# One load of 32 KB rows for the keys of unit 1 in the first and the last pair, instead of two of 16 KB rows

## The chip, the cores and the metric

The kernel runs on one core of a Trainium2 chip. A core has five engines with a queue of instructions each: TensorE (PE in the profile, its weight loads PEld), VectorE (DVE), ScalarE (ACT), GpSimd (POOL) and SyncE (SP). They work side by side and wait for each other by semaphores. Data comes from the chip's memory by DMA: an engine, here nearly always SP, issues a load, 16 DMA engines carry it out, and its semaphore reaches 16 when the last of them is done. The metric is the time of one execution on the device in microseconds (us), as the median of several.

## The reference

One step of attention decoding: 32 query heads share 8 key and value heads (4 queries each), over 65,536 positions with 128 elements each, in bfloat16.

```python
B, Hq, Hkv, Sq, Sk, D = 1, 32, 8, 1, 65536, 128
k = jnp.repeat(k, rep, axis=1)          # rep = 4
v = jnp.repeat(v, rep, axis=1)
scores = jnp.einsum("bhqd,bhkd->bhqk", q, k) * scale
p = _softmax(scores, axis=-1)
return jnp.einsum("bhqk,bhkd->bhqd", p, v)
```

Keys and values are 134 MB each, and each byte is used once for the four queries of its head.

## The kernel before

**Units and pairs.** The positions of a head are cut into 4 units of 16,384, so that there are 32 units. A unit lies in SBUF as 128 partitions by 128 tiles of 128 elements: each partition holds 128 consecutive positions, 32 KB per partition and 4 MB in all. Two units make a pair, p = 0 to 15. In a pair, unit n = 0 of the keys lies in the first half of `kbuf`, and unit 1 in `bbuf`, from which PE reads it; `vbuf` has room for both units of the values.

**Loads** (`sync_engine`, L393 to L447). SP issues all loads of keys and values, in order of pairs, keys before values. For pairs 1 to 13 (`WHOLE`) one load of 64 KB rows brings both units of keys into `kbuf` (L413), and POOL and ACT copy unit 1 from there to `bbuf` in pieces of 16 tiles (`copy_unit`, L204). For pairs 0, 14 and 15 the two units are loaded apart, and unit 1 goes straight to `bbuf`. In pairs 0 and 15 each of these loads is cut into pieces of `K_PIECES` tiles (`pieces`, L400; a tile is 256 bytes of a partition's row, so 64 tiles make rows of 16 KB). Each piece has its own semaphore, `kp[n][i]`; where there are no pieces, one load serves piece 0 and SP raises the other semaphores itself (`tokens`, L404). The values come in one load per pair of 64 KB rows, except in pair 0 (two of 32 KB rows) and in pair 15, where unit 1 comes in pieces of 73, 38, 13 and 4 tiles (`V_PIECES`).

Before a load SP waits until its place is free: `kfree` (L411), `bfree` (L418, for pairs 14 and 15), and `vfree` (L428), which DVE raises when PE has done the values of the pair before (L291, L303).

**PE** (`pe_pair`, L165). For each unit PE works in 16 groups of 8 tiles: it transposes a group of keys through the identity into PSUM (`pe_transposes`, L124; L132), and three groups later (`LAG`) multiplies the transposed keys by the four queries (`pe_scores`, L135; L141). DVE evicts three of four transposed groups from PSUM to `ktb` (L202), ACT the fourth (L200). The stream runs on from unit 0 into unit 1 without a break: the last scores of unit 0 stand behind the first transposes of unit 1. At the first group of a piece PE takes that piece's semaphore (L126, L127). After both units follow the values, 128 matmuls each (`pe_values`, L146; L159), unit 0 and then unit 1. In the last pair a correction matmul adds the accumulated sum ahead of tile 73 of unit 1 (L152).

**Between scores and values** DVE takes a maximum per partition and POOL one over the partitions, ACT computes the exponentials (L342), and DVE rescales the running sum and adds the values of a unit when PE has done them (L254).

The lines that the change bears on, of the kernel before:

```python
K_PIECES = ((64, 64), (64, 64))                                             # L23
        if j * TB in starts(K_PIECES[n]):                                   # L126, on PE
            take(pe, kp[n][starts(K_PIECES[n]).index(j * TB)], 16)
            for a, w, sm in zip(starts(sizes), sizes, sems):                # L401, on SP
                e.dma_start(to[:, a * D:(a + w) * D], s[:, a * D:(a + w) * D]).then_inc(sm, 16)
                    if p in (0, NP - 1):                                    # L420, on SP
                        pieces(to, s, K_PIECES[n], kp[n])
```

Of the kernel before, what the change touches and what calls it, by code (L numbers as in the profile page):

```python
# [19 lines left out]
Q = 32  # L20


K_PIECES = ((64, 64), (64, 64))  # L23
V_PIECES = ((128,), (73, 38, 13, 4))


# [12 lines left out]
def starts(sizes):  # L39
    return [sum(sizes[:i]) for i in range(len(sizes))]  # L40


def take(e, sem, n=1):

    e.wait_ge(sem, n)
    e.sem_inc(sem, -n)  # L46


def bass_standalone__gqa_softmax__decode_kernel(nc, q, k, v, out):
# [16 lines left out]
    def sem(name):  # L66
        return S(nc.semaphore(name))
# [36 lines left out]

    kp = [[sem(f"kp{i}_{p}") for p in range(len(K_PIECES[i]))] for i in range(2)]
    vp = [[sem(f"vp{i}_{p}") for p in range(len(V_PIECES[i]))] for i in range(2)]
# [17 lines left out]
    def pe_transposes(pe, n, j):  # L124
        kv = (bbuf if n else kbuf)[:, 0:T * D].rearrange("p (t d) -> p t d", d=D)
        if j * TB in starts(K_PIECES[n]):  # L126
            take(pe, kp[n][starts(K_PIECES[n]).index(j * TB)], 16)  # L127
        if n and j * TB % CB == 0:
# [264 lines left out]
    def sync_engine(e):  # L393
# [6 lines left out]
        def pieces(to, s, sizes, sems):  # L400
            for a, w, sm in zip(starts(sizes), sizes, sems):  # L401
                e.dma_start(to[:, a * D:(a + w) * D], s[:, a * D:(a + w) * D]).then_inc(sm, 16)  # L402
# [5 lines left out]
        for p in range(NP):  # L408
# [6 lines left out]
            else:  # L415
                for n in range(2):
# [3 lines left out]
                    if p in (0, NP - 1):  # L420
                        pieces(to, s, K_PIECES[n], kp[n])
                    else:
# [62 lines left out]
```

## Time and profile before

| what | value |
|---|---|
| median of 3 runs | 628.26 us (628.15 to 628.27) |
| the profiled execution, its own time | 628.49 us |
| its span, first to last instruction | 627.1 us |
| read from memory | 268.44 MB |
| busy share of the span: PE, DVE, ACT, POOL | 77%, 50%, 36%, 25% |
| mean granted clock of PE | 0.77 |

The profile is of one execution. Its page has the busy share of each engine in 40 equal slices of the span (a digit is tenths, 9 is 90% or more), the granted clock of PE in the same slices, a chain of waits followed back from the end, groups of instructions by line, and the DMA issues with the median time from issue to landing. The trace behind it can be asked for a timeline of one engine (start, duration, engine, line, operation, output<-inputs, count; in brackets the idle time before it and what ended it), for the DMA issues of a short stretch alone, and for stretches of time (for each engine busy time and count of instructions, then the granted clock, the DMA share and GB/s). Times of the trace count from the span's start.

### The profile page before, as it was taken

The page shows a single profiled execution, that of the slowest core. Times are in us where ns is not written, and L with a number is a line of the kernel's source. Part 1 is how long each engine was busy: PE and PEld are TensorE (multiplying, and loading weights), DVE is VectorE, ACT ScalarE, POOL GpSimd, SP SyncE. Part 2 cuts the span into 40 slices and gives each one's busy share as a digit, 9 for nine tenths or more (in the row PEclk, how much of TensorE's full clock was granted, in tenths as well). Part 3 has the DMA queues.
Part 4 walks back from the last instruction along what each step waited for, and adds up shares of the span by engine and source line. Part 5 has one row for each costly group of instructions (what it writes and reads, how often), then busy time and mean ns, then how long its engine had stood idle before and what let it go on. Part 6 is the DMA issues. An engine that isn't in the chain of part 4 may idle for free. (4 is left out here: it accounts for less than half of the span.)

```text
span 627.1 us, 27836 instructions
## 1 busy us (share of the span) xinstructions
PE 485.4 (77%) x12292; PEld 479.7 (76%) x12292; DVE 315.0 (50%) x699; ACT 228.9 (36%) x445; POOL 159.9 (25%) x124
## 2 busy tenths in 40 slices
PE   4851995949959498695976949779496895999797
PEld 4851995949859498695976949779496895999697
DVE  4620653717537174371744617356182562848283
ACT  2320542515335153341634406245071441624142
POOL 0000704307042070520605115060250702400000
PEclk9865886958869597695977959779596795969596
DMA  8999999999999999999999999999999999999997
GB/s 368 433 454 424 439 431 439 426 443 426 443 418 451 414 447 418 443 422 439 431 431 439 426 439 431 439 431 435 435 435 435 435 435 435 416 451 428 402 436 308
DMA packets 6568, 268.57 MB, mean 428 GB/s; under 512 B 928, under 2 KB 1056, under 8 KB 1184
## 3 DMA queue, kind: packets, MB, share of 16 engines
q1 hardware_dynamic: 6512, 268.45, 99.2%
q8 instruction: 6, 0.10, 0.1%
q10 hardware_dynamic: 48, 0.01, 0.0%
q14 instruction: 2, 0.02, 0.0%
HBM read 268.44 MB, written 0.01 MB: 428 GB/s over the span
## 5 line engine op out<-in xcount | busy, mean ns | idle before, releaser
L202 DVE COPY ktb<-trb 128x1024 bf16<-128x1024 bf16 x384 | 254.6, 689 | 177.3 <-PE trb L132 173.4
L132 PE MATMUL trb<-ident,kbuf 128*128 128x128 bf16 x2048 | 179.0, 246 | 105.4 <-PEq L46 105.3
L200 ACT ACTIVATE ktb<-trb 128x1024 bf16<-128x1024 bf16 x128 | 131.0, 1023 | 351.7 <-PE trb L132 297.5
L132 PEld LDWEIGHTS trb<-ident,kbuf 128*128 128x128 bf16 x2048 | 145.4, 112 | 106.4 <-issue 106.1
L208 POOL COPY bbuf<-kbuf 128x2048 bf16<-128x2048 bf16 x78 | 143.9, 1892 | 178.2 <-POOLq L46 178.2
L141 PE MATMUL qkb<-qcur,ktb 128*128 128x4 bf16 x4096 | 174.4, 165 | 11.0 <-PEq L46 10.0
L141 PEld LDWEIGHTS qkb<-qcur,ktb 128*128 128x128 bf16 x4096 | 155.8, 97 | 16.0 <-issue 16.0
L132 PE MATMUL trb<-ident,bbuf 128*128 128x128 bf16 x2048 | 157.0, 220 | 3.2 <-issue 3.2
L159 PE MATMUL pvb<-pts,vbuf 128*128 128x4 bf16 x4096 | 113.3, 166 | 15.2 <-issue 8.8
L159 PEld LDWEIGHTS pvb<-pts,vbuf 128*128 128x128 bf16 x4096 | 111.4, 103 | 16.9 <-issue 15.5
L132 PEld LDWEIGHTS trb<-ident,bbuf 128*128 128x128 bf16 x2048 | 117.3, 97 | 1.1 <-issue 1.1
L388 POOL PARTITION_ALL_REDUCE cmaxa<-cmax x32 | 11.9, 370 | 252.6 <-POOLq L46 252.6
L342 ACT ACTIVATE pts<-qkb,negm 128x128 bf16<-128x128 f32 x128 | 51.0, 549 | 37.2 <-ACTq L46 37.2
L351 ACT ACTIVATE bbuf<-kbuf 128x2048 bf16<-128x2048 bf16 x26 | 49.5, 1902 | 0.0
L342 ACT ACTIVATION_READ_ACCUMULATOR pts<-qkb,negm 128x1 f32 x128 | 35.6, 278 | 0.0
L220 DVE TENSOR_REDUCE cmax<-qkb 128x4 f32<-128x512 f32 x32 | 22.0, 686 | 23.2 <-DVEq L46 23.2
L254 DVE TENSOR_TENSOR acc<-acc,pvb 128x4 f32<-128x4 f32 x16 | 2.5, 159 | 31.2 <-PE pvb L159 31.2
L252 DVE COPY acc<-pvb 128x4 f32<-128x4 f32 x8 | 1.3, 163 | 20.1 <-PE pvb L159 20.1
L390 POOL PARTITION_ALL_REDUCE la<-lp x8 | 3.4, 430 | 30.8 <-POOLq L46 30.8
L231 DVE SCALAR_TENSOR_TENSOR negm<-cmaxa,m 128x4 f32<-128x4 f32 x24 | 3.9, 164 | 11.7 <-DVEq L46 11.5
L346 ACT ACTIVATE alpha<-dm 128x4 f32<-128x4 f32 x32 | 7.1, 221 | 0.0
L245 DVE TENSOR_TENSOR acc<-acc,alpha 128x4 f32<-128x4 f32 x24 | 3.9, 164 | 6.1 <-DVEq L46 5.7
(42 smaller groups left out, 39.0 us busy)
## 6 DMA issues: line engine op xcount, KB each, us to landing
vbuf<-in_v_dram SPq DMA_DIRECT2D x3, 4096.0 KB, 31.0
kbuf<-in_k_dram SPq DMA_DIRECT2D x4, 2048.0 KB, 16.1
bbuf<-in_k_dram SPq DMA_DIRECT2D x4, 2048.0 KB, 21.0
kbuf<-in_k_dram SPq DMA_DIRECT2D x1, 4096.0 KB, 16.3
bbuf<-in_k_dram SPq DMA_DIRECT2D x1, 4096.0 KB, 16.5
vbuf<-in_v_dram SPq DMA_DIRECT2D x1, 2336.0 KB, 27.1
vbuf<-in_v_dram SPq DMA_DIRECT2D x1, 1216.0 KB, 29.6
vbuf<-in_v_dram SPq DMA_DIRECT2D x1, 416.0 KB, 30.2
```

The costliest lines, as they stand in the source:

```text
L132: ins = pe.transpose(trb[j % NTB][:, i * P:(i + 1) * P], kv[:, t, :], ident[:, :])
L141: ins = pe.matmul(qkb[n][:, t * R:(t + 1) * R], lhsT=ktb[:, off:off + P], rhs=qcur[:, :], start=True, stop=True)
L159: ins = pe.matmul(pvb[n][:, 0:R], lhsT=vv[:, t, :], rhs=pts[n][:, t * R:(t + 1) * R], start=t == 0, stop=t == T - 1)
L200: e.activation(dst, trb[j % NTB][:, :], AF.Copy).then_inc(eva, 1)
L202: e.tensor_copy(dst, trb[j % NTB][:, :]).then_inc(evd, 1)
L208: ins = op(bbuf[:, c * CB * D:(c + 1) * CB * D], kbuf[:, off:off + CB * D])
L220: e.tensor_reduce(cmax[:, :], qkb[n][:, :].rearrange("p (t g) -> p g t", g=R), AX.X, ALU.max).then_inc(cm, 1)
L231: return e.scalar_tensor_tensor(to[:, :], cmaxa[:, :], -scale, mo[:, :], ALU.mult, ALU.min)
L342: ins = e.activation(pv[:, g, :], sv[:, g, :], AF.Exp, bias=negm[:, g:g + 1], scale=scale, accum_out=rsum[:, g:g + 1])
L346: e.activation(alpha[:, :], dm[:, :], AF.Exp, scale=1.0).then_inc(sx, 1)
L351: return e.activation(o, i, AF.Copy)
L388: e.partition_all_reduce(cmaxa[:, :], cmax[:, :], P, bass.bass_isa.ReduceOp.max).then_inc(cma, 1)
```

## The change

`K_PIECES` has one piece of 128 tiles for unit 1 instead of two of 64:

```diff
-K_PIECES = ((64, 64), (64, 64))
+K_PIECES = ((64, 64), (128,))
 V_PIECES = ((128,), (73, 38, 13, 4))
```

In pairs 0 and 15 SP issues one load of 4 MB with rows of 32 KB into `bbuf` where it issued two of 2 MB with rows of 16 KB. There is one semaphore for it, `kp[1][0]`, which PE takes ahead of the first transposes of unit 1, in every pair; the second one, which PE took ahead of group 8 of unit 1, is gone, and with it SP's increments of it in the other pairs. On SP the list of loads differs at these two places alone; the instructions of PE, DVE, ACT and POOL are in the same order.

## The prediction

> **What bounds the kernel now.** I read the page's summary first, for what is busy all the time:
>
> ```profile
> span 627.1 us, 27836 instructions
> PE   4851995949959498695976949779496895999797
> DMA  8999999999999999999999999999999999999997
> HBM read 268.44 MB, written 0.01 MB: 428 GB/s over the span
> ```
>
> The DMA row is 9 in all slices but the first and the last. PE has slices of 4 and 5 in every pair, until the last eight slices. So the load queue sets the pace, and PE can catch up with it in every pair but the last, after which no load follows that could cover it. Next I read the chain of waits, for the end:
>
> ```profile
> 585.89 6.98 PE pvb L159 x256
> ...
> 593.79 29.62 DMA vbuf<-in_v_dram
> ...
> 623.46 1.69 PE pvb L159 x55
> ```
>
> The chain says that the end waits for a V load. How near PE is to being the one that is late shows only in PE's own timeline of the last 23 us:
>
> ```profile
> 592.92 3.57 PE L132 MATMUL trb<-ident,kbuf 128*128 128x128 bf16 x32
> ...
> 604.39 0.61 PE L132 MATMUL trb<-ident,bbuf 128*128 128x128 bf16 x8
> ...
> 616.05 0.34 PE L141 MATMUL qkb<-qcur,ktb 128*128 128x4 bf16 x8 [0.52 <-PEq L46]
> 616.36 3.50 PE L159 MATMUL pvb<-pts,vbuf 128*128 128x4 bf16 x128
> 620.75 2.09 PE L159 MATMUL pvb<-pts,vbuf 128*128 128x4 bf16 x73 [0.89 <-PEq L46]
> 622.70 0.57 PE L152 MATMUL pvb<-acc,identf 128*128 128x4 f32 x2
> 623.46 1.68 PE L159 MATMUL pvb<-pts,vbuf 128*128 128x4 bf16 x55 [0.19 <-DMA vbuf<-in_v_dram]
> ```
>
> The reader is to see the 0.19 in the last row. From 592.92 on PE works without a gap that a DMA causes: both transposed units, their scores, the values of unit 0, the first 73 tiles of unit 1. It is done with them at 622.70 + 0.57 = 623.27, and waits 0.19 us for the second V piece. The kernel is bound by loads for 623 us, yet whatever delays PE in the last pair by more than 0.19 us moves the end. The two short gaps (0.52 and 0.89) end with PE's own chain (scores, maximum, exponentials, values), so they move along with a delay and don't absorb it.
>
> **The change, part by part.** Two things change: how fast the loads go, and when unit 1's keys may be read.
>
> *Loads.* Four 2 MB loads (the two halves of unit 1's keys, in pairs 0 and 15) become two of 4 MB. What one costs in the full queue is the distance of landings; landing is issue plus time to landing:
>
> ```profile
> 580.56 0.80 SPq L402 DMA_DIRECT2D bbuf<-in_k_dram  x2
> bbuf<-in_k_dram SPq DMA_DIRECT2D x1, 2048.0 KB, 19.7
> L402 SPq DMA_DIRECT2D bbuf<-in_k_dram x1: 433/433/433, 580.9 to 580.9; - x1
> bbuf<-in_k_dram SPq DMA_DIRECT2D x1, 2048.0 KB, 24.3
> 592.94 2.23 SPq L402 DMA_DIRECT2D vbuf<-in_v_dram x5
> vbuf<-in_v_dram SPq DMA_DIRECT2D x1, 4096.0 KB, 21.9
> ```
>
> The first half lands at 580.56 + 19.7 = 600.3, the second at 580.9 + 24.3 = 605.2, and the 4 MB of V unit 0 (32 KB rows, the new shape) at 592.94 + 21.9 = 614.8. A 2 MB load takes 4.9, two of them 9.8; the 4 MB load 9.6. These are rounded to 0.1, so a merged load gains between 0 and 0.2; I take 0.1, the middle. The queue is never empty between pair 0 and the end, so both gains add up: 0.1 for all that lands from pair 0 on, 0.2 from the merged load of pair 15 on. One SP issue (0.33 to 0.71 us of SP) less per pair is worth nothing: V's issue waits until 592.9 for PE's values of pair 14, and the queue then still holds keys until 605. PE also loses one wait per pair, at unit 1's transposes 8; that second half had landed at 605.2, before PE came to it, so the wait it drops held nothing up.
>
> *A rule of the skill that would make it more.* The Trainium skill (DMA: Bandwidth & Descriptors, Anatomy of one DMA) fits the time of one DMA as about 2.0 us plus its bytes over the bandwidth, for a GpSimd-issued one. By it two loads fewer would be an estimated 4 us less. The rows above disagree for queued loads: 2 MB at 428 GB/s is 4.9 us, the whole distance, and leaves no room for 2.0.
>
> *Unit 1's keys in the last pair.* PE takes one semaphore for all 128 tiles ahead of the first transposes out of `bbuf`. They started at 604.39, with the first half there since 600.3. Now they need the whole load: 605.2 - 0.2 = 605.0. To that comes the time from landing to the first matmul. The nearest rows are the first load of all, and the first transposes:
>
> ```profile
> 0.72 0.88 SPq L402 DMA_DIRECT2D kbuf<-in_k_dram  x2
> kbuf<-in_k_dram SPq DMA_DIRECT2D x1, 2048.0 KB, 7.4
> 8.29 3.57 PE L132 MATMUL trb<-ident,kbuf 128*128 128x128 bf16 x32 [2.94 <-PEq L46]
> ```
>
> Landing at 8.1, first matmul at 8.29: 0.2 us, and 0.05 to 0.3 as bounds (the last V piece landed at 623.41 in the chain, its matmul started at 623.46). So PE starts at 605.2 instead of 604.39, 0.8 later. Behind the wait on PE stand the scores of unit 0's last three groups, and after them everything to the end; DVE and ACT evict what PE had done and then wait for it. From the first of these transposes to the end of the correction matmul PE takes 623.27 - 604.39 = 18.88 us, so it is done at 605.2 + 18.88 = 624.1. The second V piece is there since 623.41 - 0.2 = 623.2 and costs no wait any more: the last 55 matmuls start at 624.1 instead of 623.46. What follows them is not touched. Sum: +0.65 us; with the load gain between 0 and 0.4 and the start between 0.05 and 0.3 it is +0.3 to +0.9 (start at 604.85 or at 605.5, each less 604.39 and less the 0.19).
>
> *Unit 1's keys in the first pair.* Here PE comes much too early:
>
> ```profile
> 1.65 1.17 SPq L402 DMA_DIRECT2D bbuf<-in_k_dram  x2
> bbuf<-in_k_dram SPq DMA_DIRECT2D x1, 2048.0 KB, 17.7
> L402 SPq DMA_DIRECT2D bbuf<-in_k_dram x1: 706/706/706, 2.1 to 2.1; - x1
> bbuf<-in_k_dram SPq DMA_DIRECT2D x1, 2048.0 KB, 22.2
> 20.12 0.61 PE L132 MATMUL trb<-ident,bbuf 128*128 128x128 bf16 x8
> 26.81 0.27 PE L132 MATMUL trb<-ident,bbuf 128*128 128x128 bf16 x1 [2.26 <-issue]
> 20.23 0.33 SPq L413 DMA_DIRECT2D kbuf<-in_k_dram  x1
> kbuf<-in_k_dram SPq DMA_DIRECT2D x1, 42.8
> 53.46 0.33 SPq L436 DMA_DIRECT2D vbuf<-in_v_dram  x1
> 0.00:5.00 5.00, 0.00 (x0) 0.00 (x0) 1.71 (x15) 1.69 (x3) 0.72 (x6) 1.00 0.62 221
> ```
>
> The first half landed at 19.4, PE began at 20.12; the whole lands at 2.1 + 22.2 - 0.1 = 24.2, and PE begins at 24.4, 4.2 later. What is late next is pair 0's values, and with them SP's V load of pair 1, issued at 53.46. It is covered by the 8 MB of pair 1's keys, which last until 20.23 + 42.8 = 63.0. From an issue to moving bytes takes 1.2 us (the first 5 us have 0.62 x 5 = 3.1 us of DMA, so it began at 1.9, issued at 0.72), so the issue is in time until 61.8: 8.3 us of cover. PE's delay is between 4.2 - 2.26 = 1.9 (the gap without work at 24.5 falls into the new wait) and 4.2 plus two windows at half clock, 1.5 each by the rows below: 7.2. That is less than 8.3, so this wait costs nothing; beyond the cover each us would reach the end in full.
>
> **The clock.** A pause can lower it, so I looked at the transposes in windows of the clock's grid:
>
> ```profile
> 23.31:26.72 3.41, 1.16 (x16) 1.00 0.98 418
> 26.72:30.13 3.41, 3.15 (x25) 0.50 1.07 461
> 30.13:33.55 3.42, 2.79 (x35) 1.00 1.07 455
> 33.55:36.96 3.41, 1.17 (x15) 1.00 1.03 444
> 470.45:473.87 3.42, 1.56 (x23) 1.00 1.06 460
> 473.87:477.28 3.41, 0.00 (x0) 0.50 1.07 461
> 603.57:606.99 3.42, 3.18 (x44) 1.00 1.11 479
> ```
>
> After windows with 16 and with 23 transposes the granted clock is 0.50; after one with 35 it stays 1.00. The window of the new wait has 44 now, and with 0.9 us of it idle (from 604.3, where PE will be, to 605.2) some 44 x 2.5 / 3.4 = 32. That is nearest to the 35, so I expect full clock. A window at half clock does 25 transposes where 44 are usual and so loses 3.41 x (1 - 25/44) = 1.5 us. The Trainium skill (TensorE: Matmul & The Clock Gate, Why this matters for your kernels) says that gaps above some 3 us throttle; by it too the last pair's short gap changes nothing, though here a gap of 2.26 us was enough.
>
> **The rivals.**
> - *Clock drop, slower.* The 0.9 us pause puts the window from 603.57 under the threshold, somewhere between 23 and 35 transposes, and the next runs at half clock, with nothing behind it to catch up: +0.65 + 1.5 = +2.15, 630.4. For it: 32 lies in the unknown gap. Against: at its far end. It decides as soon as the count falls under the threshold.
> - *Cover gone in pair 0, slower.* PE's gaps without work grow when they meet larger rows, and V of pair 1 is issued past 61.8: +0.65 and about 2 more, 630.9. Against: 8.3 of cover, where the upper bound of the delay is 7.2.
> - *The wait is hidden.* The last bytes of the one load land earlier than the distance of landings says, by 604.2, and PE doesn't stop. Then the 0.2 of the loads is all: 628.05. Against: the bytes ahead in the queue are the same, and at 428 GB/s they can't come 0.8 us sooner.
> - *Fixed cost per load, faster.* Each load has a part that its neighbours don't hide, and PE, started sooner in each pair, follows. Rows allow at most 0.2 a load, so PE's wait decides still; only the skill's 2.0 would make it 624.3.
>
> **How the numbers follow.** The profiled execution took 628.49 for a span of 627.1; the median of the other runs is 628.26, 0.23 lower. The forecast is 628.49 + 0.65 = 629.1 for a profiled execution, and 628.26 + 0.65 = 628.9 for the median. Chances: forecast 0.71, with a range of its own of 628.5 to 629.2; wait hidden 0.10; clock drop 0.12; cover gone 0.05; fixed cost 0.02. To hold 8 in 10 the range reaches from the hidden wait (628.0) to the clock drop (630.4), and leaves out the last two. 0.2% is 1.26 us, about what a measurement of this kernel can tell from no change; so the forecast and the hidden wait (0.81) count as the same, clock drop and cover gone as slower (0.17), and the fixed cost as faster (0.02).
>
> **What would show it.** In the changed kernel's profile the last pair's first transposes out of `bbuf` should start near 605.2, after an idle time put down to the DMA, and the wait of 0.19 before the last 55 matmuls should be gone. In pair 0 the same transposes start near 24.4, V of pair 1 is still issued before 61.8, and keys of pair 1 land near 62.9. The granted clock stays 1.00 from 606.99 on. I am wrong if PE starts on `bbuf` in the last pair without a wait, if V of pair 1 comes late, or if the end waits for a DMA again.

## The result, and the profile after

The changed kernel takes 630.79 us in the median of 13 executions, the kernel before 628.27 us on the same chips. The ratio of the means is 1.0034, with a 95% interval of 1.0023 to 1.0046: slower, by 2.5 us in the median. More telling than the median is the spread. Before, 13 executions lie between 628.15 and 628.43; after, between 628.11 and 632.38. The fastest is as fast as before, the slowest 4 us slower.

Three lines of the page of the changed kernel (an execution of 631.24 us), and then the end of its chain of waits:

```profile
span 629.9 us, 27804 instructions
DMA  9999999999999999999999999999999999999996
...
q8 instruction: 6, 0.10, 0.1%
...
623.82 2.09 PE pvb L159 x73
625.91 0.43 PE pvb L152 x2
626.33 1.60 PE pvb L159 x55
```

The chain has no DMA any more: PE runs from the first to the last value of unit 1 without a wait. Read alone, that supports the forecast (PE is now the late one). But 2.8 us more span isn't the 0.65 of the forecast, and most of it is there long before, in the first 90 us. SP's loads, by start, duration and count:

```profile
1.65 0.42 SPq L402 DMA_DIRECT2D bbuf<-in_k_dram  x1
...
20.64 0.33 SPq L413 DMA_DIRECT2D kbuf<-in_k_dram  x1
60.79 0.33 SPq L436 DMA_DIRECT2D vbuf<-in_v_dram  x1
```

The load of V for pair 1 is issued at 60.79, where it was 53.46 before. The time to landing of the last two of them (keys of pair 1, V of pair 1), of the kernel after:

```profile
kbuf<-in_k_dram SPq DMA_DIRECT2D x1, 42.2
vbuf<-in_v_dram SPq DMA_DIRECT2D x1, 24.1
```

and of V before:

```profile
vbuf<-in_v_dram SPq DMA_DIRECT2D x1, 29.0
```

Keys of pair 1 land at 20.64 + 42.2 = 62.8, before at 63.0. V of pair 1 lands at 60.79 + 24.1 = 84.9, before at 53.46 + 29.0 = 82.5. From the keys to the values it is 22.1 us instead of 19.4, for the same 8 MB. Something is lost between the two, and the same stretch of time in both kernels shows what (PE, PEld, DVE, ACT and POOL busy, then the clock, the DMA share and GB/s). Before:

```profile
60.40:61.80 1.40, 0.00 (x0) 0.00 (x0) 0.00 (x0) 0.00 (x0) 0.00 (x0) 0.50 0.98 421
```

After:

```profile
60.40:61.80 1.40, 0.23 (x9) 0.15 (x6) 0.16 (x1) 0.00 (x0) 0.00 (x0) 0.50 0.48 152
```

The DMA engines are half idle from 60.4 to 61.8. A window is a weak witness here, since with rows of 64 KB a row is counted where it starts. The start and length of each packet (here a row of a load) in the trace say it better: the last rows of pair 1's keys end between 60.46 and 60.91 for ten of the 16 engines, and only between 61.79 and 62.41 for the other six, which is why the load as a whole lands so late. The load issued at 60.79 moves its first row at 61.76, 0.97 us after the issue. In between the ten have nothing to do. Before, V's rows follow the keys' on every engine without a pause.

Why the issue is late, PE's timeline of pair 0 after the change says (rows with an idle time ahead, which the brackets give):

```profile
24.38 1.01 PE L132 MATMUL trb<-ident,bbuf 128*128 128x128 bf16 x8 [3.72 <-PEq L46]
...
33.01 0.22 PE L132 MATMUL trb<-ident,bbuf 128*128 128x128 bf16 x1 [2.01 <-issue]
...
41.20 0.55 PE L132 MATMUL trb<-ident,bbuf 128*128 128x128 bf16 x7 [1.76 <-issue]
...
51.28 3.54 PE L159 MATMUL pvb<-pts,vbuf 128*128 128x4 bf16 x127 [5.22 <-issue]
58.48 0.27 PE L159 MATMUL pvb<-pts,vbuf 128*128 128x4 bf16 x4 [3.66 <-issue]
```

Before, beside the row at 26.81 with its 2.26:

```profile
34.07 0.56 PE L132 MATMUL trb<-ident,bbuf 128*128 128x128 bf16 x7 [0.95 <-issue]
...
43.89 3.52 PE L159 MATMUL pvb<-pts,vbuf 128*128 128x4 bf16 x127 [4.97 <-issue]
51.09 0.28 PE L159 MATMUL pvb<-pts,vbuf 128*128 128x4 bf16 x5 [3.68 <-issue]
```

PE starts on `bbuf` at 24.38, as forecast, but the gaps without a cause in the profile ("issue"), which sum to 11.9 us before (2.26, 0.95, 4.97, 3.68), aren't swallowed by the new wait: 12.7 us in these rows. And the clock was lowered, as two windows of PE show (busy time and count, then the clock, the DMA share and GB/s):

```profile
20.00:24.30 4.30, 0.66 (x17) 0.86 0.90 389
24.30:30.00 5.70, 5.62 (x84) 0.51 1.02 443
```

Before, the second of these windows had

```profile
24.30:30.00 5.70, 3.44 (x54) 0.71 1.07 457
```

### The profile page after: what moved, and what is told of

Same layout as the page of the kernel before. It is cut to its first block, busy times and chain, and to the rows that moved or that the text cites. A ratio compares the mean times of both kernels' runs of the same rounds, so it can differ in the third digit from the quotient of the medians.

```text
span 629.9 us, 27804 instructions
## 1 busy us (share of the span) xinstructions
PE 488.4 (78%) x12292; PEld 482.6 (77%) x12292; DVE 315.3 (50%) x699; ACT 228.9 (36%) x445; POOL 159.9 (25%) x124
## 5 line engine op out<-in xcount | busy, mean ns | idle before, releaser
L132 PE MATMUL trb<-ident,bbuf 128*128 128x128 bf16 x2048 | 159.0, 221 | 8.2 <-PEq L46 4.4
L132 PEld LDWEIGHTS trb<-ident,bbuf 128*128 128x128 bf16 x2048 | 119.1, 98 | 6.4 <-issue 6.4
## 6 DMA issues: line engine op xcount, KB each, us to landing
vbuf<-in_v_dram SPq DMA_DIRECT2D x1, 2336.0 KB, 27.1
```

What stands on the lines that cost most here:

```text
L132: ins = pe.transpose(trb[j % NTB][:, i * P:(i + 1) * P], kv[:, t, :], ident[:, :])
```

## The experiments

There were twelve runs: nine other kernels, and the changed one three times more. Where pairs 0 and 15 are told apart, PE keeps both semaphores of unit 1, and SP raises the second one itself for a single load, as the kernel does in pair 14.

**The change in the last pair alone.**

```diff
-                    if p in (0, NP - 1):
+                    if p == 0 or p == NP - 1 and n == 0:
```

> The change in the last pair alone; pair 0 keeps its two loads. Theory (pair 0's late V load makes the loss and the scatter, the last pair's wait adds a fixed part): PE's first transposes out of bbuf in the last pair move from 604.4 to about 605.3, the end by +0.7, so 629.0 us with a scatter like that of before (0.3 us). Rival 1 (the last pair's wait is hidden in runs without a profile): 628.2. Rival 2 (the last pair makes the scatter): median near 630.8, spread over 4 us.

Measured: 628.41 us (628.08 to 628.59), before on that chip 628.44; ratio 0.9999 (0.999 to 1.0008). That is the outcome of rival 1, but not for its reason: the profiled execution loses nothing either (628.48). PE's rows in its profile:

```profile
605.45 0.61 PE L132 MATMUL trb<-ident,bbuf 128*128 128x128 bf16 x8 [1.16 <-PEq L46]
...
617.42 3.41 PE L159 MATMUL pvb<-pts,vbuf 128*128 128x4 bf16 x128
621.05 2.08 PE L159 MATMUL pvb<-pts,vbuf 128*128 128x4 bf16 x73 [0.22 <-PEq L46]
623.00 0.57 PE L152 MATMUL pvb<-acc,identf 128*128 128x4 f32 x2
623.48 1.68 PE L159 MATMUL pvb<-pts,vbuf 128*128 128x4 bf16 x55
```

The wait is there, 1.16 us, and everything behind it is 1.06 us later up to 617.42. Then the gap ahead of the 73 tiles, 0.89 before, is 0.22, and the one ahead of the 55 is gone. The last 55 start at 623.48, before at 623.46. So the two waits for V pieces together took the whole delay, 0.76 us at the first piece and 0.28 at the second.

**What ended the gap of 0.89.** The kernel before, with smaller first values in the last pair:

```diff
-V_PIECES = ((128,), (73, 38, 13, 4))
+V_PIECES = ((128,), (48, 63, 13, 4))
```

> The kernel before with the values of unit 1 of the last pair in pieces of 48, 63, 13 and 4 tiles instead of 73, 38, 13 and 4. It asks what ends PE's gap of 0.89 us between the values of unit 0 and unit 1 in the last pair. Theory (the landing of the first V piece, 2.4 us earlier with 48 tiles): the gap shrinks to about 0.2 and values of unit 1 start near 620.1. Rival, as the prediction had it (PE's own chain of scores, maximum and exponentials): the gap stays at 0.9.

Measured: one execution of 629.14 us (the second piece is now larger, and PE waits longer for it). The gap is 0.16 (the values start at 620.39 and not near 620.1, as PE was 0.4 us later all through the last pair of this execution):

```profile
616.77 3.46 PE L159 MATMUL pvb<-pts,vbuf 128*128 128x4 bf16 x128
620.39 1.42 PE L159 MATMUL pvb<-pts,vbuf 128*128 128x4 bf16 x48 [0.16 <-PEq L46]
```

It was a DMA's. The profile of before has it, too, if one looks for the landing:

```profile
593.31 0.43 SPq L402
```

```profile
vbuf<-in_v_dram SPq DMA_DIRECT2D x1, 2336.0 KB, 27.1
```

The first row is the issue of the piece of 73 tiles in the chain of waits, the second its time to landing: 593.31 + 27.1 = 620.4, just ahead of PE's 620.75. "PEq" in the bracket names PE's own queue; it doesn't say that the wait was for PE's own work (the wait of 1.16 for the keys, above, has it too). ACT's exponentials of unit 1 were done at 619.8.

**The change in pair 0 alone.**

```diff
-                    if p in (0, NP - 1):
+                    if p == NP - 1 or p == 0 and n == 0:
```

> The change in pair 0 alone; the last pair keeps its two loads. Theory: SP issues V of pair 1 near 60.8 us instead of 53.5, DMA engines run dry, and the time scatters from 628 to 632 with a median near 630.1 (the change's 630.8 less the last pair's 0.65). Rival (the last pair makes the loss): 628.2 with a scatter of 0.3.

Measured: 630.68 us (629.76 to 631.37, 5 executions), ratio 1.0039 (1.0026 to 1.0053). The whole loss, and a spread of 1.6 us in five executions, come with pair 0 alone. V of pair 1 is issued at 60.53 in its profile.

**The same wait with rows of 16 KB.** In pair 0 the half that PE needs first is loaded second:

```diff
+                    if p == 0 and n == 1:
+                        for i in (1, 0):
+                            e.dma_start(to[:, i * W // 2:(i + 1) * W // 2],
+                                        s[:, i * W // 2:(i + 1) * W // 2]).then_inc(kp[1][i], 16)
```

> Pair 0 keeps two loads of 16 KB rows for unit 1, in the other order: the half that PE needs first is loaded second, so PE waits as long as with one load; last pair as before. Theory (the wait counts, not the rows): the same as pair 0's change alone, median near 630.2 with a scatter of some us. Rival (larger rows hold up other transfers): 628.3 and no scatter, V of pair 1 issued well before 60.

Measured: 630.93 us (628.54 to 631.5, 6 executions), ratio 1.0028 (1.0014 to 1.0042); V of pair 1 issued at 60.75. The larger rows aren't needed for the loss; PE's wait is enough.

**A queue that has work while PE is late.** Pair 0's change, and V of pair 1 in two loads; DVE raises `vhalf` when unit 0's values are done:

```diff
+        e.sem_inc(vhalf, 1)
...
+            if p == 1:
+                e.wait_ge(vhalf, 1)
+                e.dma_start(vbuf[:, 0:W], vs[:, 0:W]).then_inc(vp[0][0], 16)
```

> Pair 0's change alone, and V of pair 1 comes in two loads, unit 0 as soon as PE has done the values of unit 0 of pair 0, so that the DMA queue has work while PE is late. Theory: the queue doesn't run dry, the scatter is gone, 628.2 us (0.1 less than before by the larger rows). Rival (the loss comes from PE being late as such, or from the larger rows): as pair 0's change alone, near 630 with scatter.

Measured: 628.49 us (628.23 to 628.81), ratio 0.9999 (0.999 to 1.0008). SP's two loads in its profile:

```profile
53.43 0.33 SPq L430 DMA_DIRECT2D vbuf<-in_v_dram  x1
60.82 0.33 SPq L440 DMA_DIRECT2D vbuf<-in_v_dram  x1
```

PE ends pair 0 as late as in the changed kernel (its second load is issued at 60.82), and nothing is lost. So PE's delay costs nothing by itself; the empty queue does.

**The whole change with the two loads of V.** The same edit on the changed kernel.

> The whole change (one load of 32 KB rows in both pairs), and V of pair 1 in two loads, unit 0 issued as soon as PE has done unit 0's values of pair 0. Theory (a dry DMA queue between pair 1's keys and values is the whole loss, the last pair's wait is free): no scatter, 628.3 us, V of pair 1 issued near 53 and 61 us. Rival (some of the loss is left elsewhere): above 629.

Measured: 628.35 us (628.12 to 628.5), ratio 0.9998 (0.9989 to 1.0007). The change's loss is gone. The forecast gain of 0.1 to 0.2 from the merged loads can't be told from nothing: before on that chip was 628.47, and the interval is some 0.6 us to either side.

**The late load without the change.** The kernel before; SP waits ahead of V of pair 1 for a signal that DVE gives at the first group of each pair:

```diff
+                e.sem_inc(vgo, 1)
...
+            if p == 1:
+                e.wait_ge(vgo, 2)
```

> The kernel before, nothing merged, with SP's V load of pair 1 held back until DVE has the first transposed group of pair 1, near 64 us. Theory (the late issue alone makes the loss, whatever the rows and PE's waits): issued 3 to 4 us later than in the change's profile (60.8, which cost 1.3 to 2.8), so 4 to 6 us above before: 632.5 to 634.5 us, with less scatter as the issue is tied to the landing of pair 1's keys. Rival (PE's wait or the larger rows are needed for the loss): below 630.

Measured: 633.18 us (633.15 to 633.48), ratio 1.0077 (1.0062 to 1.0093), issued at 64.59. A late load alone makes the loss. Here the issue is tied to a landing, and the spread is 0.3 us; that fits a spread of the change that comes from when V is issued, but the table below shows that the issue isn't all of it.

**How much wait pair 0 bears.** Unit 1's keys in pieces of 96 and 32, and of 112 and 16 tiles, in the first and the last pair:

```diff
-K_PIECES = ((64, 64), (64, 64))
+K_PIECES = ((64, 64), (96, 32))
```

> Unit 1's keys of the first and last pair in pieces of 96 and 32 tiles: PE needs 96 tiles ahead of unit 1, which land 2.4 us before the whole. Theory: in pair 0 PE starts on bbuf near 22 us, V of pair 1 is issued near 56 to 58 us, before the queue is empty at 60.5, so 628.4 and no scatter. Rival (any wait in pair 0 costs in proportion): about 1 us above before.

> The same with pieces of 112 and 16 tiles, which land 1.2 us before the whole. Theory: V of pair 1 is issued between 58 and 60.5 us, at the edge: some executions like before, some up to 2 us longer; median between 628.4 and 630. Rival (proportional): about 2 us above before.

Measured: 628.48 us (628.24 to 628.76, ratio 1.0001, 0.9992 to 1.001) with 96, and 628.49 us (628.33 to 631.32, ratio 1.0006, 0.9997 to 1.0015) with 112, where ten executions are like before and one is 2.8 us longer. V of pair 1 is issued at 55.80 and 55.91 in their profiles. The expectation for 112 (58 to 60.5) missed, and that for 96 (56 to 58) by a little: the issue doesn't move in proportion to the wait.

**The changed kernel three times more**, for issue and time of the same execution.

> The changed kernel again, for one more pair of V's issue time in pair 1 and time of the whole. Theory: issued before about 59.5 us it costs nothing (628.2 to 628.5); issued later, DMA engines stand empty before the V load and the span grows by 1 to 4 us. Rival (the loss doesn't hang on this issue): no order between the two.

> As the run before it: one more pair of issue time and time of the whole, with the same expectations.

> As the two runs before it: one more pair of issue time and time of the whole, with the same expectations.

Measured: 628.38, 630.69 and 630.62 us. With the profiled executions of the other kernels:

| kernel | V of pair 1 issued, us | it lands | span, us |
|---|---|---|---|
| before | 53.46 | 82.5 | 627.1 |
| changed, second profile (`after_b`) | 55.64 | 82.4 | 627.0 |
| last pair alone | 56.16 | 82.5 | 627.1 |
| pair 0 alone | 60.53 | 83.6 | 628.4 |
| changed, fourth (`after_d`) | 60.55 | 84.6 | 629.3 |
| changed, third (`after_c`) | 60.65 | 84.7 | 629.3 |
| pair 0, halves swapped | 60.75 | 84.9 | 630.1 |
| changed, first | 60.79 | 84.9 | 629.9 |
| before, V held back | 64.59 | 86.5 | 631.8 |

Up to 56.2 the issue costs nothing; at 60.5 to 60.8 it costs 1.3 to 3.0 us of span; at 64.6, 4.7. V's landing is late by nearly the same amount (1.1 to 2.4, and 4.0), and the rest of the kernel never makes it up. The issue scatters without the change, too: pair 0 is the same code in "before" and "last pair alone", and V is issued 2.7 us apart. The execution with the early issue, `after_b`, has one gap fewer on PE:

```profile
24.07 1.01 PE L132 MATMUL trb<-ident,bbuf 128*128 128x128 bf16 x8 [3.94 <-PEq L46]
32.01 0.26 PE L132 MATMUL trb<-ident,bbuf 128*128 128x128 bf16 x1 [1.84 <-issue]
41.92 0.34 PE L141 MATMUL qkb<-qcur,ktb 128*128 128x4 bf16 x8 [0.68 <-PEq L46]
46.13 3.55 PE L159 MATMUL pvb<-pts,vbuf 128*128 128x4 bf16 x127 [2.00 <-issue]
```

The gap that stands at 41.20 in the first profile is missing, and the next is 2.00 instead of 5.22, so PE is 5.15 us ahead from there on. In its four profiles the same kernel therefore issues once near 55.6, and then takes as long as before, and three times near 60.7, and then takes 2.2 to 2.8 us more. The 13 executions of the result, with 628.72, 629.55 and 630.02 among them, don't fall into two groups so cleanly.

## Why the prediction was wrong

The forecast was 628.9 for the median, with a range of 628.0 to 630.4, and 630.79 was measured: the last pair was charged 0.65 that it didn't cost, and pair 0 nothing where it cost some 2.5.

**The bound.** Right: the load queue sets the pace, and a delay of the queue in pair 1 reaches the end whole. (The PE row was read a little too neatly: not every pair has a 4 or a 5, and the last 5 stands seventh from the end; nothing hangs on it.)

**The loads.** Right as far as it shows: by the semaphores' times, keys of pair 1 land at 62.76 to 63.32 us in the seven profiles with one load in pair 0 (mean 62.97) and at 63.04 to 63.19 in the seven with two (mean 63.11), so 0.14 earlier, where 0.1 was forecast, within a scatter of 0.6. With the loss taken away (`after_vsplit`) the kernel is no slower than before; the gain itself is too small for the interval of the times. The 2.0 us per load of the Trainium skill (DMA: Bandwidth & Descriptors, Anatomy of one DMA) didn't show, in line with the rows that spoke against it.

**Unit 1's keys in the last pair: wrong, +0.65 predicted, nothing measured.** The wait came as worked out (with the last pair alone keys land at 605.16 and PE starts at 605.45, where 605.0 and 605.2 were forecast, with 605.5 as the upper bound; the wait is 1.16 us there, 0.71 in the first profile of the change). The step that failed is the sentence that the two short gaps "end with PE's own chain". The 0.52 did; the 0.89 ended with a V piece, which lands at 620.4 whatever PE does. PE's slack in the last pair was therefore not 0.19 but near 1: with the last pair alone PE is 1.06 late at 617.42, 0.30 late at 621.05 after the first V piece, and 0.02 late at 623.48 after the second.

**Unit 1's keys in the first pair: wrong, nothing predicted, about all of the loss measured.** The step that failed is the comparison of delay and cover, "less than 8.3, so this wait costs nothing", and in it the cover.

The delay was sized nearly right: 1.9 to 7.2 us were given, 60.79 - 53.46 = 7.33 was measured in the first profile, 7.07 to 7.29 in the four others that lost time over this wait, 2.18 in `after_b`. Only its lower bound was wrong: the gap of 2.26 was to fall into the new wait, but 2.01 and 1.76 came again behind it. Of the 7.39 us that PE is late at 51.28 (43.89 before), 4.26 are the later start on `bbuf`, 0.8 are longer gaps (9.7 us instead of 8.9, with the short one ahead of the last scores) and the remaining 2.3 are slower work between them, with the clock lowered.

The cover is what was mis-sized. The 8.3 us were counted to the landing of the last bytes of pair 1's keys, 63.0. But a load lands when the slowest of 16 DMA engines is done, and ten of them run empty between 60.5 and 60.9. From issue to first row it is 0.97 us here (0.96 to 0.97 in the five profiles with an issue at 60.53 to 60.79), not 1.2. So the last issue that leaves no engine empty is an estimated 60.5 - 0.97 = 59.5, and the cover 59.5 - 53.46 = 6.0 us: less than the delay. An issue at 60.79 lost 2.4 us of landing, though it lay 1.0 us ahead of the 61.8 that was given as its limit. Where between 56.2 and 60.5 the cost begins wasn't tried, so the 59.5 isn't shown by a time.

**The rivals.** What happened is *cover gone in pair 0*, to which 0.05 was given. Its place and its outcome were right (V of pair 1 comes too late for the queue), and its price (about 2 us) near the 1.3 to 3.0 measured. Its cause wasn't: the gaps grew by 0.8 us only, and the swapped halves lose as much without larger rows. Its point of decision, 61.8, was wrong, and the word "against" rested on that. That its 630.9 lies beside the measured 630.79 is in part luck, as 0.65 of it is the last pair's, which cost nothing. *Clock drop* didn't come in the last pair: the change's window with the wait had 33 transposes, that of the last pair alone 27, and both were followed by full clock. First the changed kernel, then the last pair alone (transposes only; busy time and count, then the clock):

```profile
606.79:610.20 3.41, 2.40 (x33) 1.00 1.03 442
610.20:613.62 3.42, 3.22 (x44) 1.00 1.05 450
```

```profile
602.84:606.25 3.41, 1.97 (x27) 1.00 0.94 404
606.25:609.66 3.41, 3.21 (x46) 1.00 1.05 452
```

So the line that was bounded by 23 and 35 lies below 27. Counts of transposes don't draw it sharply: a window with 24 was followed by half clock in `after_b` (from 28.17) and by full clock in `k96_32` (from 470.03). In pair 0 the clock did fall, to 0.51, and is part of the delay.

**Left open.** PE's gaps without a cause go with the loading of its program. The page's row of the queue for instructions has 6 packets of 16 KB, and the trace has their times. In the kernel before four of them end at 25.31, 32.78, 42.60 and 49.64, and PE goes on at 26.81, 34.07, 43.89 and 51.09; in the changed kernel they end at 31.54, 39.94, 49.84 and 57.02, and PE goes on at 33.01, 41.20, 51.28 and 58.48. In all 14 profiles each such gap of 0.4 us or more ends 1.3 to 1.6 us after such a packet, though not each packet ends a gap. That is agreement in time, in every profile; no run moved the packets, so it isn't shown by an experiment. What sets the time of a packet, and so what makes an execution issue near 55.6 or near 60.7, is open.

The price at nearly one issue time, 1.3 to 3.0 us, goes with the engine that comes to V last: its first row starts at 62.56 before, at 63.20 where 1.3 is lost, and at 63.74 to 64.06 where 2.2 to 3.0 are. What holds that engine up is open.

## What to carry to other kernels

A wait that seems covered has to be measured against the moment at which the first DMA engine runs empty, less the time from an issue to its first row (0.97 us here), not against the landing of the last byte, and the delay it makes has to be carried on to the next issue that hangs on the delayed engine. Where a stall may come from a queue that runs dry, what helped here was to hand the next load over in parts, each as soon as its own place is free. And a wait whose releaser the profile gives as the engine's own queue is to be compared with the landings of the loads it takes, before it is called the engine's own work.

## What the runs showed of the hardware

A load that finds engines of the queue empty costs more than the time for which they were empty. Issued at 60.53 to 60.79, with ten of 16 engines run empty between 60.5 and 61.2 and the first row moving at 61.49 to 61.76, V of pair 1 landed 1.1 to 2.4 us late; the first row of each engine took 2.9 to 3.0 us in the mean, where 2.42 is usual. PE lost 7.5 us (`after_b`) to 15.0 us (`first_vsplit`) in pair 0 to gaps with no cause in the profile, 11.9 before, 14.4 with the last pair alone. The Trainium skill (Runtime: NRT & Kernel Launch, Instruction fetch mechanics) says that an engine's program is refilled in 16 KiB blocks and that crossing to a new one is mostly hidden; if the gaps are these refills, as the times of the packets suggest, this case disagrees, with gaps of up to 6.2 us beside a full DMA queue.
